# A transformer block with a Fourier mixer: the second norm of half the rows beside the feed-forward, the first norm's scale in the weights, another order of steps

## The chip, the cores and the metric

The kernel runs on one core of a Trainium2 chip. It is one launch; its time is the device time of that core in microseconds. The core's engines are TensorE (PE: matmuls, and loads of the stationary operand, PEld), VectorE (DVE), ScalarE (ACT), GpSimd (POOL) and SyncE (SP), which here only issues DMAs. Each works through its own list of instructions in order and waits on semaphores for the others. The compared number is the median of several runs; beside it there is one profiled execution, from which all durations below come.

## The reference

The block has 2048 rows (sequence) of 512 columns (hidden), and a feed-forward of 1792:

```python
mod = (silu(c) @ w_mod).reshape(1, 6, 1, -1)
sa, ca, ga, sb, cb, gb = (mod[:, i] for i in range(6))
h = layernorm(x) * (1 + ca) + sa
a = einsum("bsd,ed->bse", h, dft_hid_re); b = einsum("bsd,ed->bse", h, dft_hid_im)
y = einsum("ts,bse->bte", dft_seq_re, a) - einsum("ts,bse->bte", dft_seq_im, b)
x = x + ga * y
h = layernorm(x) * (1 + cb) + sb
out = (silu(h @ w1) * (h @ w3)) @ w2          # 512 -> 1792 -> 512
x = x + gb * out
```

All is fp32. The DFT matrices are inputs like the others.

## The kernel before

**Arithmetic.** Every matmul operand is split into a high part, rounded for TensorE's fast fp32 form, and a low rest (names ending in h and l), and a product is made of three passes: high by high, low by high, high by low. `product` (line 99) issues them. The DFTs use the matrices' mirror symmetry: sums and differences of mirrored rows and columns halve them. The matrices are inputs, so the kernel also compares the given matrices with the entries that it relies on; these are the "checks", whose loads are named cx, cy, cz, cv, and whose steps run beside other work; a general path behind a branch is there for other matrices and is not taken. The feed-forward's products are made with seven block products in place of eight: "units" a1 to a7 (w1) and b1 to b7 (w3) on the operands h2h, h2l and the block sums th, tl, and on block sums of the weights (w1s, w3s), each split again.

**Stages.** (1) The first layernorm of eight groups of row pairs k: statistics, scale, transposes by TensorE (`turn_rows`, line 712), then the modulation with 1 + ca and sa (`modulate_rows`, lines 725 and 727, on ACT or DVE: hm), mirror sums and differences (`mirror_sums`: hs, on DVE or POOL), their split (hh, hl), and the hidden DFT (`hid_product` line 805, `hid_difference` line 821), whose results are split into us and ul. (2) The sequence DFT (`seq_piece` line 1169, `seq_lines` line 1199) over four blocks of rows, with m, the matrix's pieces, split into mh and ml. The results of the odd and the even halves are read into od and ev; uv are the odd halves' sums. (3) For each of the four blocks: the gate ga, the additions to x (`odd_add`, `add_rows`: xa, xb), the statistics (`ln2_stats`), the root and scale (xn), transposes of x and of xn by TensorE into PSUM banks (`turn_block`, line 1346), a copy of the transposed x to DRAM (`keep_sums`: xm), and the modulation of the transposed xn (`modulate_block`: xc), from which h2h, h2l, th and tl are made. (4) The feed-forward: 14 items (g, pair), g a seventh of the 1792 columns, pair 0 the blocks 0 and 1, pair 1 the blocks 2 and 3; each item has 14 factor units and 8 down units of six matmuls of 512 columns, so 132 matmuls, 1848 in all. Beside each item ACT and DVE make silu and product (v, hf), read the down products (y), and split the next weights (w, w1s, w1l, w3s, w3sl and so on).

**What sets the order.** Stages 1 to 3 and the first units of 4 are `task`s: a name, a rank, needs, slots, and the engines that could do it, with a cost each. `arrange` is a list scheduler that runs when the program is built: again and again it takes, among the steps that could begin soonest by its own costs, the one of lowest rank. The tables `KIND_BY` and `STEP_BY` shift ranks by kind and by step. Large tiles lie in a pool of 50 slots; `take` gets the slot that was given back first, `give` returns one. From there on the loop over the items writes the order: units in a fixed pattern (a6, a5, y, y, ...), and behind each unit `beside` spends credits of DVE and ACT time on three queues, `jobs`, `background` and `checks`, in this order; `drain` works a queue off until something that is needed is there. The down products and other short uses of PSUM alternate between two banks. `look` starts the check loads (not with fewer than SPARE slots free, nor in paused items) and takes their steps LAG calls later.

## Time and profile before

| | us |
|---|---|
| median of 3 runs | 667.55 (666.27 to 671.1) |
| profiled execution | 672.04 |
| its span (first to last instruction) | 670.2 |
| mean granted TensorE clock in it | 0.958 |
| busy PE / DVE / ACT / POOL | 612.2 / 524.2 / 374.5 / 233.7 |

How to read the rows: a group's row names the line, the engine, the operation, output <- inputs, shapes and count, then busy time and mean duration in ns, then the engine's idle time ahead of the group and what ended it. A row of the chain of waits is start, duration, engine, output and line. A row of windows is the stretch, its length, then busy time and count of PE, PEld, DVE, ACT and POOL, the granted clock as a fraction, the DMA engines' busy share, and GB/s; where it is asked for one line of the program, only the engines that this line uses are there. "L99" is line 99 of the kernel.

### The profile page before, as it was taken

The page shows a single profiled execution, that of the slowest core. Times are in us where ns is not written, and L with a number is a line of the kernel's source. Part 1 is how long each engine was busy: PE and PEld are TensorE (multiplying, and loading weights), DVE is VectorE, ACT ScalarE, POOL GpSimd, SP SyncE. Part 2 cuts the span into 40 slices and gives each one's busy share as a digit, 9 for nine tenths or more (in the row PEclk, how much of TensorE's full clock was granted, in tenths as well). Part 3 has the DMA queues.
Part 4 walks back from the last instruction along what each step waited for, and adds up shares of the span by engine and source line. Part 5 has one row for each costly group of instructions (what it writes and reads, how often), then busy time and mean ns, then how long its engine had stood idle before and what let it go on. Part 6 is the DMA issues. An engine that isn't in the chain of part 4 may idle for free.

```text
span 670.2 us, 8742 instructions
## 1 busy us (share of the span) xinstructions
PE 612.2 (91%) x2893; PEld 500.4 (75%) x2893; DVE 524.2 (78%) x1014; ACT 374.5 (56%) x591; POOL 233.7 (35%) x252
## 2 busy tenths in 40 slices
PE   6989789999766989999999999997999999999975
PEld 3889778767544778778888888786878788887854
DVE  5898764999997655869787767797888899889462
ACT  5577564632558666465564757574656466565310
POOL 7875108248534014241522101321443335431000
PEclk7999998999769999999999999998999999999988
DMA  7662037943033529997999566898999999997004
GB/s 254 196 195 80 1 94 191 276 130 126 0 125 127 189 45 262 241 269 204 231 248 254 100 125 125 214 196 190 246 250 270 267 245 269 242 277 200 25 16 114
DMA packets 61872, 119.15 MB, mean 178 GB/s; under 512 B 10681, under 2 KB 29113, under 8 KB 61820
## 3 DMA queue, kind: packets, MB, share of 16 engines
q1 hardware_dynamic: 45228, 67.92, 35.5%
q0 software_dynamic: 13824, 47.98, 32.0%
q10 hardware_dynamic: 2768, 2.62, 1.3%
q8 instruction: 24, 0.39, 0.2%
q14 instruction: 28, 0.23, 0.1%
HBM read 85.99 MB, written 35.65 MB: 182 GB/s over the span
## 4 chain that ended last, share of the span: by engine, by line
PE 57%; DVE 16%; issue 8%; DMA 7%; ACT 6%; POOL 5%; SPq 0%; POOLq 0%; DVEq 0%; ACTq 0%
PE banks L99 40%; PE banks L1169 6%; DMA sum<-y 3%; PE banks L1199 2%; DMA cz<-in_ctr 2%; PE banks L821 2%; PE banks L805 1%; DMA w<-in_w 1%; DVE cj L1534 1%; DVE x L87 1%; POOL cy L273 1%; DMA lt<-dt 1%; PE banks L1346 1%; ACT th L81 1%; PE banks L1061 1%
## 5 line engine op out<-in xcount | busy, mean ns | idle before, releaser
L99 PE MATMUL banks<-hf,w2h 128*128 128x512 f32 (+1 forms) x452 | 142.5, 395 | 7.0 <-ACT hf L81 3.4
L1714 POOL DMA_DIRECT2D sum<-y x48 | 45.3, 953 | 216.9 <-ACT y L598 197.6
L99 PEld LDWEIGHTS banks<-hf,w2h 128*128 128x128 f32 x452 | 85.6, 191 | 28.5 <-DVE hf L84 4.3
L99 PE MATMUL banks<-hf,w2l 128*128 128x512 f32 (+1 forms) x226 | 88.6, 392 | 0.0
L598 ACT ACTIVATE y<-banks,gb 128x512 f32<-128x512 f32 x96 | 65.1, 682 | 20.8 <-PE banks L99 16.9
L81 ACT ACTIVATE hf<-v 128x512 fp32r<-128x512 f32 x56 | 35.4, 632 | 73.5 <-DVE v L90 67.8
L81 ACT ACTIVATE x<-banks 128x512 f32<-128x512 f32 x84 | 48.5, 590 | 21.8 <-PE banks L99 21.2
L87 DVE TENSOR_TENSOR x<-banks,x 128x512 f32<-128x512 f32 x42 | 28.9, 688 | 34.9 <-PE banks L99 28.2
L1798 ACT ACTIVATE v<-v 128x512 f32<-128x512 f32 x42 | 26.4, 629 | 49.8 <-DVE v L87 49.6
L99 PEld LDWEIGHTS banks<-hf,w2l 128*128 128x128 f32 x226 | 43.1, 191 | 8.7
L87 DVE TENSOR_TENSOR v<-banks,x 128x512 f32<-128x512 f32 x42 | 28.8, 687 | 17.7 <-PE banks L99 17.7
L84 DVE TENSOR_TENSOR hf<-v,hf 128x512 fp32r<-128x512 f32 x56 | 38.4, 685 | 2.5 <-ACT hf L81 2.3
L99 PE MATMUL banks<-tl,w1sh 128*128 128x512 f32 x84 | 33.3, 396 | 0.2 <-DVE tl L93 0.2
L99 PE MATMUL banks<-th,w1sh 128*128 128x512 f32 x84 | 33.2, 396 | 0.0
L99 PE MATMUL banks<-th,w1sl 128*128 128x512 f32 x84 | 33.2, 395 | 0.0
L99 PE MATMUL banks<-th,w3sh 128*128 128x512 f32 x84 | 32.9, 392 | 0.2 <-ACT x L81 0.2
L99 PE MATMUL banks<-th,w3sl 128*128 128x512 f32 x84 | 32.7, 389 | 0.0
L99 PE MATMUL banks<-tl,w3sh 128*128 128x512 f32 x84 | 32.7, 389 | 0.0
L90 DVE TENSOR_TENSOR v<-v,x 128x512 f32<-128x512 f32 x42 | 29.2, 695 | 1.4
L538 PE MATMUL banks<-tmp 128*128 128x128 f32 (+1 forms) x182 | 26.9, 300 | 3.1 <-DVE tmp L428 3.1
L805 PE MATMUL banks<-wu,hh 128*128 128x256 f32 x128 | 25.3, 296 | 3.7 <-ACT ho L81 2.4
L273 POOL DMA_INDIRECT cv<-in_cti,mirror x16 | 18.0, 1126 | 28.6 <-PE banks L99 23.9
(349 smaller groups left out, 1704.8 us busy)
## 6 DMA issues: line engine op xcount, KB each, us to landing
sum<-y POOLq DMA_DIRECT2D x48, 512.0 KB, 7.7
w<-in_w SPq DMA_DIRECT2D x42, 512.0 KB, 5.9
wmc<-in_wmc SPq DMA_DIRECT2D x8, 512.0 KB, 7.3
sum<-xm SPq DMA_DIRECT2D x8, 512.0 KB, 3.3
cx<-in_ctr SPq DMA_DIRECT2D x16, 256.0 KB, 10.1
cz<-in_ctr SPq DMA_DIRECT2D x16, 256.0 KB, 10.2
cx<-in_cti SPq DMA_DIRECT2D x16, 256.0 KB, 14.2
cz<-in_cti SPq DMA_DIRECT2D x16, 256.0 KB, 8.2
```

Of the source, the lines that this page charges most:

```text
L81: nc.scalar.activation(dst, src, AF.Copy, scale=scale)
L84: nc.vector.tensor_tensor(out=dst, in0=a, in1=b, op=OP.subtract)
L87: nc.vector.tensor_tensor(out=dst, in0=a, in1=b, op=OP.add)
L90: nc.vector.tensor_tensor(out=dst, in0=a, in1=b, op=OP.mult)
L99: nc.tensor.matmul(acc, lhs[a], rhs[b], start=first and n == 0, stop=last and n == len(PASSES) - 1, skip_group_check=more,)
L273: nc.gpsimd.indirect_dma_start(dst, None, src, bass.IndirectOffsetOnAxis(ap=at, axis=0))
L538: nc.tensor.matmul(warm[:, :width], onesf[:, :P], onesf[:, :width], start=True, stop=True)
L598: nc.scalar.activation(dst, src, AF.Identity, scale=by)
L805: nc.tensor.matmul(halves(hb[k])[:, m, :], sides((hh, hl)[a][k])[:, dt, m, :], wu[dt][:, b, m, :], start=False, stop=dt % 2 == 1 and n == ...
L1169: nc.tensor.matmul(acc(b, m), (mh, ml)[p][b, o][:, m, cols(a)], (us, ul)[q][k][:, m, :], start=(o, a, n) == (0, 0, 0), stop=False, skip_gr ...
L1714: nc.gpsimd.dma_start(sums[t, d // 2], y, accum_op=OP.add)
L1798: behind(k != 0 or q == 0, lambda: nc.scalar.activation(v, src, AF.Silu))
```

## The change

Five things are changed together.

*Order.* `take` gets the slot that comes free earliest by the planner's time, and `arrange` reckons with it: a step that needs a slot is not planned before the soonest slot is left. `drain` charges costs. Both tables of ranks are new (23 kinds in place of 45, 18 steps in place of some 60).

*First norm.* The scale 1 + ca goes into the hidden DFT's weights: `w_highs`, `w_lows` and the new `round_differ` multiply by a column of mod1. The shift sa becomes a row: `shift_product`, eight matmuls of 97 x 512, a few small splits (qs, qt), and `hid_shift` and `hid_share` add it into the hidden DFT's banks; the side products of lines and rows get a term each. `modulate_rows` is gone; `own_rows` copies one half of the transposed rows from PSUM, and `mirror_sums` takes the other from PSUM, on DVE alone.

*Second norm's sums.* `add_rows` runs as scalar_tensor_tensor on 512 columns with an accumulated sum; the mean is taken from it, ACT squares the centred row with a second sum, and the root divides by D. `ln2_stats` is gone.

*Blocks 2 and 3.* Their norm, from the loads of the rows to the modulated transposes, is a list of steps in `background`, beside the first items. Transposes go in groups of four, each into the next of the two down banks, and ACT reads them.

*Checks.* LAG is 7 instead of 9, SPARE 7 instead of 6 and two more until block 3 is done; loads pause in item 6 alone, not in 5 and 6.

The first place is TensorE at the end of the sequence DFT. Before, the last of L1199 is followed by transposes and a few units (L99):

```order
L1199 MATMUL banks<-ya_243,er_1283 128x512
L1199 MATMUL banks<-ya_243,sel_329 128x512
...
L1346 MATMUL banks<-ident,xn_1819 128x128 x2
L1346 MATMUL banks<-anti,xn_1821 128x128 x2
L99 MATMUL banks<-h2h_1854,w1h_1564 128x512
...
L1346 MATMUL banks<-ident,xa_1649 128x128 x2
L1346 MATMUL banks<-anti,xb_1650 128x128 x2
L99 MATMUL banks<-th_2060,w1sh_1598 128x512
```

After, the normalized rows of block 1 (xn) are turned ahead of the last piece (L1256, L1286), and only transposes of x (xa, xb) and the first units (L106) follow:

```order
L1435 MATMUL banks<-ident,xn_1691 128x128 x2
L1435 MATMUL banks<-anti,xn_1708 128x128 x2
L1256 MATMUL banks<-us_921,mh_1640 128x512
...
L1286 MATMUL banks<-ya_244,er_1226 128x512
L1286 MATMUL banks<-ya_244,sel_323 128x512
...
L1435 MATMUL banks<-anti,xb_1181 128x128 x2
L106 MATMUL banks<-h2h_1749,w1h_1570 128x512
...
L106 MATMUL banks<-h2h_1763,w1l_1597 128x512
L1435 MATMUL banks<-ident,xa_1384 128x128 x2
```

The transposes of xn of blocks 0 and 1 have moved ahead of the end; of blocks 2 and 3 none is left here.

The second place is the third item of the feed-forward, on TensorE and ScalarE (th, tl, h2h, h2l are operands of factor units, hf of down units). On TensorE block 2's transposes now stand between the units:

```order
L106 MATMUL banks<-tl_1892,w3sh_2371 128x512
L106 MATMUL banks<-th_1888,w3sl_2373 128x512
L1435 MATMUL banks<-ident,xn_2451 128x128 x2
L1435 MATMUL banks<-anti,xn_2462 128x128 x2
L106 MATMUL banks<-hf_2336,w2h_2238 128x512 x2
...
L106 MATMUL banks<-hf_2290,w2l_2240 128x512
L1435 MATMUL banks<-ident,xn_2451 128x128 x2
L1435 MATMUL banks<-anti,xn_2462 128x128 x2
L106 MATMUL banks<-th_1896,w3sh_2371 128x512
...
L106 MATMUL banks<-th_1896,w3sl_2373 128x512
L1435 MATMUL banks<-ident,xn_2451 128x128 x2
L1435 MATMUL banks<-anti,xn_2462 128x128 x2
L106 MATMUL banks<-h2h_1749,w1h_2412 128x512
```

On ScalarE the root of block 2, with a load of its table ahead and another behind the modulations, now stands among x, y, hf and v of the feed-forward:

```order
L88 ACTIVATE hf_2487<-v_2299 128x512
L621 ACTIVATE y_2489<-banks,gb 128x512
L1414 ACT_TABLE_LOAD
L1414 ACTIVATE ln_2383<-ln_2383,eps 128x4
L88 ACTIVATE x_2460<-banks 128x512
L88 ACTIVATE x_2516<-banks 128x512
...
L1467 ACTIVATE xc_2568<-banks,sb,cb_234 128x512 x2
L1929 ACT_TABLE_LOAD
L1929 ACTIVATE v_2563<-v_2563 128x512
```

Before, no transpose of a second norm and no table load stands in this item; the one load stood ahead of the first v. The third place is ScalarE at the end of the hidden DFT. Before, the copy ho of the last pair stands behind two pieces mh and their squares (junk):

```order
L81 ACTIVATE mh_1112<-m_922 128x1024
L81 ACTIVATE mh_1123<-m_1107 128x1024
L294 ACTIVATE junk_1136,chk<-mh_1123 128x512 x2
L294 ACTIVATE junk_1147,chk<-ec_934 128x1024
L81 ACTIVATE ho_1159<-banks 128x512
```

After, the second of these mh stands behind it:

```order
L88 ACTIVATE ho_1069<-banks 128x512
L88 ACTIVATE mh_1074<-m_859 128x1024
...
L88 ACTIVATE ho_1134<-banks 128x512
L88 ACTIVATE gr_1139<-banks 64x64 x2
L88 ACTIVATE us_1144<-banks 128x2x256
L88 ACTIVATE us_1168<-banks 128x2x256
L88 ACTIVATE mh_1187<-m_1085 128x1024
```

The diff, cut to its core; the two tables stand as one line of the new one, since their numbers say nothing to a reader:

```diff
     def take(dt=F32, what="s"):
-        slot = free.popleft()
+        slot = min(free, key=lambda n: left_at[n])
+        free.remove(slot)
+        taken.append(left_at[slot])
         count[0] += 1
         t = big.tile([P, 2, N], dt, name=f"{what}_{count[0]}", tag=f"slot{slot}")
         slot_of[id(t)] = (slot, t)
         return t
 
-    def give(t):
+    def give(t, after=0.0):
         slot, _ = slot_of.pop(id(t))
         free.append(slot)
+        left_at[slot] = now[0] + after
+        given.append((slot, after))
...
+            soonest = sorted(left_at[n] for n in free)
...
+                        if slots and us:
+                            begin = max(begin, soonest[0])
...
+            fn(engine) if len(ways) > 1 else fn()
+            if taken and us and max(taken) > begin:
+                begin = max(taken)
+                put(begin)
+                for slot, more in given:
+                    left_at[slot] = now[0] + more
...
-        for m, sign in enumerate((1.0, -1.0)):
-            copy(u[:, 0, m, :], r[:, m, 0, :], sign)
+        for m in range(2):
+            copy_by(u[:, 0, m, :], r[:, m, 0, :], mod1[:, 1 + m, dt : dt + 1])
...
+    def round_differ(dt):
         r = quarters(raw_w[dt])
         if dt % 2 == 0:
             wd[dt // 2] = take(F32R, "wd")
...
+        for m in range(2):
+            copy_by(
+                wd[dt // 2][:, dt % 2, m * HALF : (m + 1) * HALF], r[:, m, 1, :],
+                mod1[:, 1 + m, dt : dt + 1],
+            )
...
+    def shift_product(m, dt):
+        nc.tensor.matmul(
+            bank(6)[:97],
+            mod1[:, 0, dt : dt + 1].to_broadcast([P, 97]),
+            raw_w[dt][:, m, :],
+            start=dt == 0,
+            stop=dt == ND - 1,
+        )
...
-    def modulate_rows(k, dt, engine):
-        if k not in hm:
-            hm[k] = take(F32, "hm")
-        src = turned[k][dt // 2][:, (dt % 2) * HALF : (dt % 2 + 1) * HALF]
-        dst = four(hm[k])[:, dt, :]
-        sa, ca1 = mod1[:, 0, dt : dt + 1], mod1[:, 1, dt : dt + 1]
-        if engine == "ACT":
-            nc.scalar.activation(dst, src, AF.Identity, bias=sa, scale=ca1)
-        else:
-            nc.vector.tensor_scalar(dst, src, ca1, sa, op0=OP.mult, op1=OP.add)
-
-    def mirror_sums(k, m, engine):
-        if k not in hs:
-            hs[k] = take(F32, "hs")
-        own = sides(hm[k])[:, :, 0, :]
-        dst = sides(hs[k])[:, :, m, :]
-        tensors(engine, dst, own, sides(hm[k])[:, :, 1, :], OP.subtract if m else OP.add)
-        if k == NK // 2:
-
-            (nc.gpsimd if engine == "POOL" else nc.vector).tensor_copy(sides(hs[k])[:, :, m, 0:1], own[:, :, 0:1])
+    def turned_rows(k):
+        return banks[:, 2 * (k % 2) : 2 * (k % 2) + 2, :].rearrange(
+            "p h (t s n) -> p (h t) s n", t=2, s=2
+        )
+
+    def own_rows(k):
+        hs[k] = take(F32, "hs")
+        copy(sides(hs[k])[:, :, 0, :], turned_rows(k)[:, :, 0, :])
+
+    def mirror_sums(k, m):
+
+        first = int(k == NK // 2)
+        own = sides(hs[k])[:, :, 0, :]
+        mirrored = turned_rows(k)[:, :, 1, first:]
+        (minus if m else plus)(sides(hs[k])[:, :, m, first:], own[:, :, first:], mirrored)
+        if m and first:
+            nc.vector.tensor_copy(sides(hs[k])[:, :, 1, 0:1], own[:, :, 0:1])
...
+    def hid_shift(k, first):
+
+        nc.tensor.matmul(
+            hb[k], shift_twos(k), shift_row[:, 0, :], start=first, stop=False, skip_group_check=True
+        )
...
+    def hid_share(k, m, n):
+        nc.tensor.matmul(
+            halves(hb[k])[:, m, :], shift_ones(1) if m else shift_twos(k), shift(n),
+            start=False, stop=False, skip_group_check=True,
+        )
...
-    def add_rows(b, n, engine):
-        t = ev[b][:, n : n + 1, :].to_broadcast([P, 2, N])
-        tensors(engine, xrow[b][n], xrow[b][n], t, OP.add)
-        if n:
+    def add_rows(b, n, q):
+
+        if (n, q) == (0, 0):
+            ln[b] = small.tile([P, 4, 4], F32, name=f"ln_{b}", tag="ln")
+        row = xrow[b][n][:, q, :]
+        nc.vector.scalar_tensor_tensor(
+            row, ev[b][:, n, :], 1.0, row, op0=OP.mult, op1=OP.add,
+            accum_out=ln[b][:, 0, 2 * n + q : 2 * n + q + 1],
+        )
+        if (n, q) == (1, 1):
...
-    def ln2_stats(b, n):
-        if n == 0:
-            ln[b] = (
-                small.tile([P, 4, 2], F32, name=f"lmv_{b}", tag="lmv"),
-                small.tile([P, 2, 4], F32, name=f"lrs_{b}", tag="lrs"),
-            )
-        st = small.tile([P, 6], F32, name=f"lst_{b}_{n}", tag="st")
-        nc.vector.bn_stats(st, xrow[b][n // 2][:, n % 2, :])
-        nc.vector.bn_aggr(ln[b][0][:, n, :], st)
+    def ln2_mean(b):
+        nc.vector.tensor_scalar(ln[b][:, 1, :], ln[b][:, 0, :], -1.0 / D, None, op0=OP.mult)
+
+    def ln2_square(b, n):
+        if n % 2 == 0:
+            xn[b, n // 2] = take(F32, "xn")
+        nc.scalar.activation(
+            xn[b, n // 2][:, n % 2, :], xrow[b][n // 2][:, n % 2, :], AF.Square,
+            bias=ln[b][:, 1, n : n + 1], scale=1.0, accum_out=ln[b][:, 2, n : n + 1],
+        )
 
     def ln2_root(b):
-        mv, r = ln[b]
-        nc.scalar.activation(r[:, 0, :], mv[:, :, 1], AF.Sqrt, bias=eps, scale=1.0)
+        r = ln[b]
+        nc.scalar.activation(r[:, 2, :], r[:, 2, :], AF.Sqrt, bias=eps, scale=1.0 / D)
...
+    def block_steps(b, next_bank):
+
+        def run(slots, dve, act, fn, *args):
+            step(background, slots, lambda: fn(*args), dve, act)
+
+        run(6, 0.0, 0.0, load_rows, b)
+        background.extend([PAUSE] * 4)
+        for n in range(2):
+            run(1 - n, 0.7, 0.0, odd_pair, b, n, "DVE")
+        run(0, 1.2, 0.0, odd_gates, b, "DVE")
+        for n in range(2):
+            run(0, 0.7, 0.0, odd_add, b, n, "DVE")
+        run(0, 1.2, 0.0, all_gates, b, "DVE")
+        if b == NT - 1:
+            run(0, 0.0, 0.0, lambda: give(gar.pop(0)))
+        for n in range(4):
+            run(0, 0.8, 0.0, add_rows, b, *divmod(n, 2))
+        run(0, 0.2, 0.0, ln2_mean, b)
+        for n in range(4):
+            run(3 - n, 0.0, 0.7, ln2_square, b, n)
+        run(0, 0.0, 0.3, ln2_root, b)
+        run(0, 0.3, 0.0, ln2_inverse, b)
+        for n in range(4):
+            run(0, 0.0 if n % 2 else 0.6, 0.8 if n % 2 else 0.0, ln2_scale, b, n, ("DVE", "ACT")[n % 2])
+        for what in "nx":
+            for i in range(2):
+                for q in range(2):
+                    to = []
+
+                    def turn_one(what=what, i=i, q=q, to=to):
+                        to.append(next_bank())
+                        turn_block(b, what, i, q, to[0])
+
+                    def read_one(what=what, i=i, q=q, to=to):
+                        (keep_sums if what == "x" else modulate_block)(b, i, q, to[0])
+
+                    run(1 - q, 0.0, 0.0, turn_one)
...
+                    run(1 - q, 0.0, 0.8 if what == "n" else 0.6, read_one)
...
+        "add": 3, "check": -16, "eq": 51, "ex": -13, "gr": 6, "gtt": 56, "hl": 9, "jw": -7,
...
+            task(f"qm{m}.{dt}", r + dt, ["modr", f"w{dt}", *before], lambda m=m, dt=dt: shift_product(m, dt), PE=0.93)
...
-        task(f"wh{dt}", -8 + 2 * dt - 26.6, [f"w{dt}"], lambda dt=dt: w_highs(dt), 1, ACT=0.73)
+        task(f"wh{dt}", -8 + 2 * dt - 26.6, [f"w{dt}", "modr"], lambda dt=dt: w_highs(dt), 1, ACT=0.83)
...
-    for b in range(NT):
-        r = begun + (24 if b < 2 else 48) + 3 * (b % 2)
+    for b in range(2):
+        r = begun + 24 + 3 * b
...
+    for b, what in ((0, "n"), (1, "n"), (0, "x"), (1, "x")):
+        r = begun + 24 + 3 * b + (30 if what == "x" else 0)
+        for i in range(2):
+            pair = 4 if (what, i) == ("n", 0) else 6
+            needs = [f"add{b}.{n}" for n in range(4)] if what == "x" and not i else [f"sc{b}.{n}" for n in range(4)]
+            needs += pair_of.get(pair, ["rowr1"] if pair == 4 else ["yc", "rowr5"])
...
-    LAG, AHEAD, SPARE = 9, 6, 6
+    LAG, AHEAD, SPARE = 7, 6, 7
     clock, begun_at, paused = [0], {}, []
+
+    def spare():
+        return SPARE if ("xc", NT - 1) in done else SPARE + 2
 
     def look(force=False):
         clock[0] += 1
-        while to_load and "lt" in done and not paused and (len(free) > SPARE or force) and len(begun_at) < AHEAD:
+        while to_load and "lt" in done and not paused and (len(free) > spare() or force) and len(begun_at) < AHEAD:
...
+    def next_bank():
+        turn[1] += 1
+        return bank(down_banks[(turn[1] - 1) % len(down_banks)])
+
+    for b in range(2, NT):
+        block_steps(b, next_bank)
...
-        paused[:] = [i] if turning - 2 <= i < turning else []
+        paused[:] = [i] if turning - 1 <= i < turning else []
```

349 lines of the change are left out of this document (193 added, 156 removed), and 17 rows, old and new, of the table STEP_BY.

## The prediction

> **What bounds the kernel now.** I read the page's head first, then the busy time of each engine in four stretches cut where the work changes, then the chain of waits around the cuts.
>
> ```profile
> span 670.2 us, 8742 instructions
> ...
> PE 612.2 (91%) x2893; PEld 500.4 (75%) x2893; DVE 524.2 (78%) x1014; ACT 374.5 (56%) x591; POOL 233.7 (35%) x252
> ```
>
> ```profile
> core 0: us, PE busy (x) PEld busy (x) DVE busy (x) ACT busy (x) POOL busy (x), PEclk, DMA share, GB/s
> 0.00:175.20 175.20, 157.93 (x903) 131.43 (x903) 142.03 (x292) 97.32 (x179) 95.70 (x131) 0.94 0.52 148
> 175.20:220.07 44.87, 28.19 (x137) 22.03 (x137) 36.81 (x51) 31.41 (x40) 17.02 (x8) 0.77 0.30 108
> 220.07:662.50 442.43, 426.09 (x1853) 346.94 (x1853) 345.23 (x672) 245.80 (x373) 121.02 (x113) 0.99 0.81 198
> ```
>
> PE (TensorE) is busy 91% of the span. Up to 175.20 us stand the first norm, the hidden DFT and the sequence DFT; from 220.07 us to 662.50 us stands the feed-forward, where PE hardly rests. Between them lie 44.87 us in which PE is busy for 28.19 us, and at a granted clock of 0.77. The same stretches for the feed-forward's matmuls alone (line 99), then for the transposes of the second norm alone (line 1346), say what PE did there:
>
> ```profile
> 175.20:220.07 44.87, 9.15 (x25) 5.52 (x25) 0.77 0.30 108
> 220.07:662.50 442.43, 423.54 (x1829) 343.96 (x1829) 0.99 0.81 198
> ```
>
> ```profile
> 0.00:175.20 175.20, 1.09 (x8) 0.86 (x8) 0.94 0.52 148
> 175.20:220.07 44.87, 20.56 (x112) 16.63 (x112) 0.77 0.30 108
> 220.07:662.50 442.43, 1.25 (x8) 0.92 (x8) 0.99 0.81 198
> ```
>
> Only 25 feed-forward matmuls are done in the gap; 112 of the 128 transposes are. The chain of waits has the price of both at full clock, and what opens the feed-forward:
>
> ```profile
> 155.08 1.02 PE banks L1346 x8
> ...
> 218.80 1.24 DVE tl L93
> ...
> 299.84 125.68 PE banks L99 x552
> ```
>
> A transpose is 1.02/8 = 0.128 us, a feed-forward matmul 125.68/552 = 0.2277 us. So the gap holds 25 x 0.2277 + 112 x 0.128 = 20 us of PE work in 44.87 us. The rest are waits for the DVE (VectorE) and ACT (ScalarE), as the PE's timeline shows (idle time ahead in brackets), and the clock that goes down with them:
>
> ```profile
> 178.29 0.47 PE L1346 MATMUL banks<-ident,xn 128*128 128x128 f32 x1 [3.12 <-DVE xn L1340]
> ...
> 191.44 0.79 PE L99 MATMUL banks<-h2l,w1h 128*128 128x512 f32 x1 [3.48 <-DVE h2l L93]
> ```
>
> **The gap.** After the change blocks 2 and 3 have no second norm here, and on PE the 32 normalized transposes of blocks 0 and 1 stand before the end of the sequence DFT (rows of the PE order above). What is left for PE between that end and the steady feed-forward is 32 transposes of x, 32 x 0.128 = 4.1 us, and the 25 matmuls, 5.7 us. I add 3 us for waits: two of the x groups reuse a bank pair that ACT must copy first, a copy of about 1 us as the ACT row at 214.36 us below shows, and the first operand once more. That makes 12.8 us where 44.87 us stood: **-32.1**. The 24 transposes (32, where 8 stand now) that go into the sequence DFT lengthen it by 24 x 0.128: **+3.1**.
>
> This needs the DVE to be ready. These groups stand on it between the hidden DFT and the feed-forward:
>
> ```profile
> L1315 DVE BATCH_NORM_STATS2 lst<-xa 128x6 f32<-128x512 f32 x8 | 5.4, 672 | 0.0
> L1315 DVE BATCH_NORM_STATS2 lst<-xb 128x6 f32<-128x512 f32 x8 | 5.3, 663 | 0.0
> L1316 DVE BATCH_NORM_AGGREGATE lmv<-lst 128x2 f32<-128x6 f32 x16 | 2.9, 182 | 0.6
> L93 DVE TENSOR_TENSOR xb<-xb,ev 128x1024 f32<-128x1024 f32 x4 | 7.0, 1762 | 0.1
> L93 DVE TENSOR_TENSOR xa<-xa,ev 128x1024 f32<-128x1024 f32 x2 | 4.6, 2298 | 0.7 <-POOL ev L93 0.6
> L1340 DVE TENSOR_SCALAR xn<-xb,lrs 128x512 f32<-128x512 f32 x4 | 2.1, 542 | 0.1
> L607 DVE SCALAR_TENSOR_TENSOR wmc<-wmc,scr 128x512 f32<-128x512 f32 x16 | 12.6, 824 | 5.5 <-PE banks L1061 5.2 <-DMA wmc<-in_wmc 0.3
> ```
>
> All of the first five go, 25.2 us. Instead come 8 additions with a sum as by-product for blocks 0 and 1. The trace has no such form with an accumulator; the nearest is line 607's at 0.824 us, so 6.6 us. That is 18.6 us less. Of nine scalings like line 1340's six stay, 1.6 us less: about 20 us. If the DVE alone set the pace, the feed-forward would open near 200 us. But it was idle for 44.87 - 36.81 = 8.1 us in the gap itself, waiting for others, and the xa and xb additions took 1.8 to 2.3 us while POOL (GpSimd) worked beside them, which the new form, on DVE alone, shortens. So I take PE's sum and keep 20 us as the other end.
>
> **Beside the feed-forward.** 64 transposes go in and 8 come out: 56 x 0.128 = **+7.2**, since PE is full there. They come in 16 groups of four; each takes a bank of the down products and must be read by ACT before the bank is free. The nearest groups of four now are line 1484's, four of them; the dearest are line 1346's, eight groups for xn:
>
> ```profile
> L1484 PE MATMUL banks<-ident,dl 128*128 128x128 f32 x16 | 2.8, 294 | 1.8 <-ACT y L598 1.2 <-ACT dt L81 0.7
> L1346 PE MATMUL banks<-ident,xn 128*128 128x128 f32 x32 | 8.3, 343 | 10.0 <-ACT xm L81 3.4 <-DVE xn L1340 3.1 <-ACT xc L1375 2.2
> ```
>
> That is 1.8/4 = 0.45 us or 10.0/8 = 1.25 us a group, or nothing where the bank has long been read: 0 to 20 us. The groups are placed between units, with 6 to 12 matmuls (1.4 to 2.7 us) to the next use, so I take half of the nearest row: **+3.6**.
>
> The root now splits the feed-forward's activations, with two table loads for each of blocks 2 and 3. The one load at the start of the feed-forward reads:
>
> ```profile
> 214.36 1.02 ACT L81 ACTIVATE xm<-banks 128x1024 f32<-128x1024 f32 x1 [0.24 <-PE banks L1346]
> 215.41 1.28 ACT L1798 ACT_TABLE_LOAD   x1
> 216.70 0.63 ACT L1798 ACTIVATE v<-v 128x512 f32<-128x512 f32 x1
> ```
>
> Four loads are 5.1 us of ACT, of which it has 442.43 - 245.80 = 197 us free; but an x, a y or a silu queued behind a load is late by 1.28 us, and PE waits for those. I take 0.5 us each: **+2**, ends 0 and 5.1. [...]
>
> The rest of the two blocks' norm lies over the first five items (5 x 132 x 0.2277 = 150 us). By the forms above it is about a dozen DVE instructions of 0.55 to 1.2 us a block, some 9 us, and as many on ACT, some 10 us. The DVE's 97 us of idle time between 220 and 662 us and ACT's 197 us are the cover. If it is gone, the DVE's 18 us show. The changed lag, spare slots and pause of the loads I cost at nothing: they act on idle times of the kind below.
>
> **The start.** The first norm's modulation goes:
>
> ```profile
> L725 ACT ACTIVATE hm<-banks,mod 128x256 f32<-128x256 f32 x18 | 9.1, 556 | 3.1 <-DVE hm L727 2.9 <-PE banks L712 0.2
> L727 DVE TENSOR_SCALAR hm<-banks,mod 128x256 f32<-128x256 f32 x14 | 7.2, 537 | 0.9 <-issue 0.5 <-ACT hm L725 0.3
> L81 ACT ACTIVATE ho<-banks 128x512 f32<-128x512 f32 x8 | 4.8, 596 | 3.0 <-PE banks L805 2.7
> L93 DVE TENSOR_TENSOR hs<-hm 128x512 f32<-128x512 f32 x11 | 7.8, 718 | 0.2
> L538 PE MATMUL banks<-tmp 128*128 128x512 f32 x6 | 4.5, 902 | 3.1 <-DVE tmp L428 3.1
> ```
>
> ACT loses 9.1 us and gains 8 copies like the third row's, 4.8 us, and 8 roundings of weight differences, by the first row's 0.556 us at most 4.4 us; the DVE loses 7.2 us and gains five mirror sums that POOL did, 5 x 0.718 = 3.6 us. The eight shift products are fp32 with 512 columns, as the last row's, and so at most 8 x 0.9 = 7.2 us of PE, but they stand where the same line 538 now fills PE's waits. The weights' high parts have to wait for the modulation vector now. And one knot is undone. Here ACT waits for a DMA with the odd DFT piece's mh and holds back the hidden product's copy ho; PE then stands:
>
> ```profile
> 93.81 1.06 ACT L81 ACTIVATE mh<-m 128x1024 fp32r<-128x1024 f32 x1 [3.87 <-DMA m<-in_cti]
> ...
> 97.95 0.50 PE L805 MATMUL banks<-wu,hh 128*128 128x256 f32 x2 [2.19 <-ACT ho L81]
> ```
>
> In the new ACT order that copy comes ahead of that mh. Between +7 us (the shift products' 7.2 us all on the path) and -11 us (the DVE's 7.2 us of modulation and the 3.87 us of the wait, both whole) I take **-4**, nearest to the knot.
>
> **Sum.** The profiled execution took 672.04 us, 0.67% over the 667.55 us median. 672.0 - 4 - 32.1 + 3.1 + 7.2 + 3.6 + 2 = 651.8 us; times 667.55/672.04, **647 us** as a median.
>
> **The rivals.** *The feed-forward pays it back.* Each group waits 1.25 us and each load is bare: 672.0 - 4 - 32.1 + 3.1 + 7.2 + 20 + 5.1 = 671.3, as median 667 us. For it: ACT is in order, and one row of it holds root, scales, modulation and reads behind each other. Against it: line 1484's groups. Chance 0.15.
>
> *The DVE sets the start.* The gap shrinks by 20 us only: 672.0 - 4 - 20 + 3.1 + 7.2 + 3.6 + 2 = 663.9, as median 659 us. For it: the DVE has 36.81 us of the gap's 44.87. Chance 0.13.
>
> *The start gives 11 us, and the late weight load shown below goes too*, 3.7 us, since loads pause in one item instead of two: 672.0 - 11 - 32.1 + 3.1 + 7.2 + 3.6 + 2 - 3.7 = 641.1, as median 637 us. For it: the first stage hangs on chains through ACT and DVE, and both get shorter. Against it: neither is busy all of the time there, so a saving need not show. Chance 0.13.
>
> *Late weights: slower.* What PE waits for in the middle of the feed-forward, and the DVE's wait behind it:
>
> ```profile
> PE banks L99 <- DVE x L87: 3.7, 1, 3.7
> ```
>
> ```profile
> 456.34 0.42 DVE L93 TENSOR_TENSOR w3s<-w 128x256 f32<-128x256 f32 x1 [3.17 <-DMA w<-in_w]
> ```
>
> ```profile
> 460.00:480.00 20.00, 20.00 (x83) 16.34 (x82) 17.75 (x40) 11.53 (x18) 6.63 (x6) 0.91 1.00 224
> ```
>
> The new code keeps two more slots back from the check loads until block 3 is done and puts two blocks' rows, six slots each, beside the weights; the DMA is at 0.81 of its time there. If a weight comes late in each of the first seven items, PE loses 3.7 us and, at clock 0.91 over 20 us, 1.8 us more: 5.5 x 7 = 38 us, giving 690 us, as median 685 us. It decides from (672.0 - 651.8)/7 = 2.9 us an item. Against it: one such wait is all the present trace has, and it lies where the loads were paused for two items. Chance 0.06.
>
> *It does not do what it says*, the blocks' norm being drained in one piece: the order has its transposes one group at a time between units. Chance 0.01, at the first rival's time.
>
> **Numbers.** The likeliest case has 0.52. The range runs from 632 us (the third rival without its 3.6 us of bank waits and 2 us of loads) to 664 us (the first rival but for its last 3 us). About 1%, some 6.7 us, is what a measurement here can tell from no change: faster is below 660.9 us, slower above 674.2 us. Faster: 0.52 + 0.13 of the third rival + 0.09 of the second, which lies close to the bound, + 0.06 of the first = 0.80; same: the rest, 0.14; slower: 0.06.
>
> **What would show it.** The steady feed-forward should begin some 9 to 13 us after the last sequence line product, near 180 us, with the granted clock at 1.0 between them; 16 groups of transposes should stand in the feed-forward with less than 0.5 us of PE idle time each; four more table loads of 1.28 us; no batch-norm statistics after the first norm's; the copy ho of the last pair without the DMA wait ahead of it. [...] I would be wrong if PE waits for the DVE's tl as at 218.80 us, or if the wait for y and x beside the new groups adds up to more than 20 us.

## The result, and the profile after

| | before | after |
|---|---|---|
| median | 668.66 us (666.27 to 671.1, 4 runs) | 710.09 us (709.3 to 714.24, 4 runs) |
| ratio, 95% interval | | 1.0632 (1.0572 to 1.0691) |
| profiled execution | 672.04 us | 710.69 us |
| its span, granted clock | 670.2 us, 0.958 | 708.9 us, 0.948 |

The change makes the kernel 6.3% slower; 647 us was forecast. Below, "before" without more is the kernel before, measured on the same chip as the run beside it. Two lines of the profile's page of after come first, and then its windows, cut at the last sequence line product and at the steady feed-forward:

```profile
span 708.9 us, 8674 instructions
...
PE 626.9 (88%) x2865; PEld 502.9 (71%) x2865; DVE 522.4 (74%) x1003; ACT 390.9 (55%) x631; POOL 221.9 (31%) x244
```

```profile
0.00:182.26 182.26, 162.23 (x900) 131.05 (x901) 147.59 (x284) 111.17 (x208) 86.49 (x123) 0.94 0.45 128
182.26:193.79 11.53, 7.37 (x47) 5.78 (x46) 8.21 (x9) 7.26 (x8) 6.19 (x3) 1.00 0.63 210
193.79:702.40 508.61, 457.31 (x1921) 366.10 (x1921) 366.57 (x712) 272.51 (x416) 129.22 (x119) 0.95 0.73 183
```

The gap did what the forecast said: 11.53 us at clock 1.00 where 44.87 us stood. The stage ahead of it ends 7.06 us later (182.26 for 175.20). The loss is in the feed-forward: 508.6 us for 442.4. PE's idle time in it is 508.61 - 457.31 = 51.3 us, for 442.43 - 426.09 = 16.3 us before, and the clock is 0.95 where it was 0.99. The rows below say what PE waits for there: the engine and line waited for, then the total, the number of waits and the longest in us:

```profile
PE banks L106 <- ACT hf L88: 11.6, 3, 5.6
PE banks L106 <- ACT x L88: 10.4, 7, 3.2
PE banks L1435 <- DVE xn L1430: 7.6, 2, 4.0
PE banks L1435 <- ACT xc L1467: 5.9, 4, 1.5
PE banks L1435 <- ACT xm L88: 4.5, 3, 1.9
```

The three rows of line 1435 are the transposes of blocks 2 and 3: 18.0 us. The other two, hf and x, are the feed-forward's own. The waits of DVE and ACT in the feed-forward say what stands behind these; neither row is in the same list of before:

```profile
DVE cj L1665 <- DMA cy<-in_ctr,mirror: 20.9, 5, 5.3
ACT hf L88 <- DMA sum<-y: 12.0, 2, 6.3
```

The first row holds checks whose indirect load has not landed. They stand on DVE ahead of the sums and products x and v, from which ACT makes hf; and in ACT's list y and x come behind that hf. So a check, which nobody is in a hurry for, stops PE. One of the five is shown here on DVE, ACT and PE in turn:

```profile
502.10 1.19 DVE L1665 SCALAR_TENSOR_TENSOR cj<-cx,cy 128x992 f32<-128x992 f32 x1 [5.35 <-DMA cy<-in_ctr,mirror]
```

```profile
506.47 0.63 ACT L88 ACTIVATE hf<-v 128x512 fp32r<-128x512 f32 x1 [5.30 <-DVE v L97]
507.00 0.67 ACT L621 ACTIVATE y<-banks,gb 128x512 f32<-128x512 f32 x1
507.57 0.59 ACT L88 ACTIVATE x<-banks 128x512 f32<-128x512 f32 x1
```

```profile
508.21 0.79 PE L106 MATMUL banks<-th,w3sh 128*128 128x512 f32 x1 [3.18 <-ACT x L88]
```

The second row is hf's slot: `take` gave one whose last tile, a y, the DMA had not yet added to its sum in DRAM. Its longest wait, 6.3 us, ends at 654.90 us, and PE's longest for hf, 5.6 us, ends behind it at 655.59 us.

**A group's wait, step by step.** ScalarE of after, at the root of block 3:

```profile
341.43 0.71 ACT L1407 ACTIVATE xn<-xb,ln 128x512 f32<-128x512 f32 x1
342.04 0.19 ACT L1407 ACTIVATION_READ_ACCUMULATOR xn<-xb,ln 128x1 f32 x1
342.25 1.28 ACT L1414 ACT_TABLE_LOAD   x1
343.55 0.30 ACT L1414 ACTIVATE ln<-ln,eps 128x4 f32<-128x4 f32 x1
...
348.95 0.69 ACT L621 ACTIVATE y<-banks,gb 128x512 f32<-128x512 f32 x1 [1.18 <-PE banks L106]
349.54 0.77 ACT L1467 ACTIVATE xc<-banks,sb,cb 128x512 f32<-128x512 f32 x1
```

DVE behind it, and PE, which stood at the transposes from 340.94 us:

```profile
343.87 0.18 DVE L1418 RECIPROCAL ln<-ln 128x4 f32<-128x4 f32 x1 [1.66 <-ACT ln L1414]
...
344.29 0.55 DVE L1430 TENSOR_SCALAR xn<-xa,ln 128x512 f32<-128x512 f32 x1
```

```profile
344.98 0.67 PE L1435 MATMUL banks<-ident,xn 128*128 128x128 f32 x2 [4.04 <-DVE xn L1430]
350.36 0.69 PE L1435 MATMUL banks<-ident,xn 128*128 128x128 f32 x2 [1.45 <-ACT xc L1467]
358.63 0.44 PE L1435 MATMUL banks<-ident,xn 128*128 128x128 f32 x2 [1.51 <-ACT xc L1467]
```

The sum, the table load, the root, the reciprocal and the scaling are issued back to back, and PE's list has the transposes right behind: 4.04 us. The later groups wait for their bank. The two banks of the down products are used in turn by units (read as y) and groups (read as xc), and the xc of one group is issued behind the next y: 0.69 + 0.77 = 1.46 us, about what PE waits in the last two rows.

### The profile page after: what moved, and what is told of

Its sections match the earlier page's. It is cut to its first block, busy times and chain, and to the rows that moved or that the text cites. A ratio compares the mean times of both kernels' runs of the same rounds, so it can differ in the third digit from the quotient of the medians.

```text
span 708.9 us, 8674 instructions
## 1 busy us (share of the span) xinstructions
PE 626.9 (88%) x2865; PEld 502.9 (71%) x2865; DVE 522.4 (74%) x1003; ACT 390.9 (55%) x631; POOL 221.9 (31%) x244
## 5 line engine op out<-in xcount | busy, mean ns | idle before, releaser
L106 PE MATMUL banks<-hf,w2h 128*128 128x512 f32 (+1 forms) x452 | 147.2, 407 | 18.7 <-ACT hf L88 11.6
L106 PEld LDWEIGHTS banks<-hf,w2h 128*128 128x128 f32 x452 | 87.7, 197 | 40.9 <-ACT hf L88 12.8
L106 PE MATMUL banks<-hf,w2l 128*128 128x512 f32 (+1 forms) x226 | 90.8, 402 | 0.0
L106 PEld LDWEIGHTS banks<-hf,w2l 128*128 128x128 f32 x226 | 44.6, 197 | 9.3
L106 PE MATMUL banks<-th,w3sh 128*128 128x512 f32 x84 | 35.4, 422 | 9.7 <-ACT x L88 9.7
L106 PE MATMUL banks<-th,w1sh 128*128 128x512 f32 x84 | 34.9, 416 | 1.5 <-ACT th L88 0.8
L106 PE MATMUL banks<-tl,w1sh 128*128 128x512 f32 x84 | 34.4, 409 | 1.1 <-DVE tl L100 1.1
L106 PE MATMUL banks<-th,w3sl 128*128 128x512 f32 x84 | 34.7, 413 | 0.0
L1665 DVE SCALAR_TENSOR_TENSOR cj<-cx,cy 128x992 f32<-128x992 f32 x16 | 19.1, 1191 | 21.1 <-DMA cy<-in_ctr,mirror 20.9
L106 PE MATMUL banks<-tl,w3sh 128*128 128x512 f32 x84 | 34.5, 411 | 0.0
L106 PE MATMUL banks<-th,w1sl 128*128 128x512 f32 x84 | 34.3, 408 | 0.0
L106 PEld LDWEIGHTS banks<-th,w3sh 128*128 128x128 f32 x84 | 16.6, 198 | 15.7 <-ACT x L88 12.4
```

What stands on the lines that cost most here:

```text
L106: nc.tensor.matmul(acc, lhs[a], rhs[b], start=first and n == 0, stop=last and n == len(PASSES) - 1, skip_group_check=more,)
L1665: nc.vector.scalar_tensor_tensor(out, a, by, b, op0=OP.mult, op1=OP.not_equal, accum_out=at)
```

## The experiments

Two theories of the 63 us between forecast and result. **A, the checks:** the lag of 7 calls, with the other spare slots and the shorter pause, lets DVE wait for loads. **B, the distance:** blocks 2 and 3's steps stand too close to each other for engines that work in order. A rival to both: the move itself, or its table loads, is what costs.

**1. The old rules of the checks.**

```diff
-    LAG, AHEAD, SPARE = 7, 6, 7
+    LAG, AHEAD, SPARE = 9, 6, 6
...
-        return SPARE if ("xc", NT - 1) in done else SPARE + 2
+        return SPARE
...
-        paused[:] = [i] if turning - 1 <= i < turning else []
+        paused[:] = [i] if turning - 2 <= i < turning else []
```

> The changed kernel with the three old rules for the checks: a check's steps 9 calls behind its load instead of 7, 6 spare slots instead of 7 and 9, loads paused in two items instead of one. Theory A (the shorter lag puts the check steps ahead of their data, and VectorE, in order, stands before them: 20.9 us of waits for cy, and behind them TensorE): the five waits for cy go, TensorE's waits at the turn of the items (3.18, 2.24, 1.94, 0.83, 1.20 and 5.55 us, 15 us) mostly go with them and with their lost clock, and the time falls by 15 to 25 us, to 685 to 695 us. Theory B (the norm of blocks 2 and 3 beside the feed-forward costs it all): no more than 5 us.

Measured: 694.45 us, 1.0392 (1.0325 to 1.0459) of before. About 16 us of the loss go, and with them the checks' wait for cy. PE's own waits change more than they shrink: in the profiled execution, the slowest of the four, PE waits 1.4 us for ACT's x where it waited 10.4, but 11.8 us for DVE's x where it waited 0.4; and ACT stands 10.3 us at one x whose slot a y's DMA still reads. Which of the three rules gives the 16 us, this run does not say.

**2. The kernel before with the new lag alone.**

```diff
-    LAG, AHEAD, SPARE = 9, 6, 6
+    LAG, AHEAD, SPARE = 7, 6, 6
```

> The kernel before, with the lag of the check steps set to 7 instead of 9 and nothing else. Theory A: VectorE waits for the checks' data here too, by 10 to 20 us, and the time rises by 8 to 20 us, to 676 to 688 us. The rival (the loads come late only because of what else the changed kernel puts on the queues): the wait stays near the 1 to 3 us of now and the time within 3 us.

Measured: 684.14 us, 1.0262 (1.0189 to 1.0334). Both waits appear in a kernel that has nothing else of the change:

```profile
DVE cj L1534 <- DMA cy<-in_ctr,mirror: 18.8, 7, 4.0
ACT hf L81 <- DMA sum<-y: 13.3, 3, 7.0
```

So the lag alone, a single number, costs 2.6%, some 17 us by the ratio and 14 us by the medians (684.14 for 670.09), where nothing else is changed. The interval lies clear of no change: A holds for its part.

**3. No table loads.** The square root of blocks 2 and 3 is left out: the identity, which needs no load, stands in its place.

```diff
-            nc.scalar.activation(r[:, 2, :], r[:, 2, :], AF.Sqrt, bias=eps, scale=1.0 / D)
+            nc.scalar.activation(r[:, 2, :], r[:, 2, :], AF.Sqrt if b < 2 else AF.Identity, bias=eps, scale=1.0 / D)
```

> The changed kernel with the root of blocks 2 and 3 left out (the same instruction with the identity instead of the square root), so that ScalarE loads no table for it: four loads of 1.28 us fewer, all else in place. If the loads hold up the chain root, scale, transposes: TensorE's waits for xn (3.58 and 4.04 us) shrink by about 1.3 us each, and with what is queued behind the loads the time falls by 4 to 10 us. If they only fill idle time of ScalarE: less than 2 us.

Measured: 705.1 us, 1.0553 (1.0484 to 1.0621), some 5 us less than after. The two intervals overlap; the runs' own times do not (702.45 to 705.66 us, and 709.3 to 714.24 us). Four loads of 1.28 us are 5.1 us, so each may be paid whole, as the forecast's upper end had it; but they are not what costs the 63 us.

**4. Distance.** A pause is an empty step: one unit of PE's work goes by. Two go ahead of the root, one between root and scaling, two ahead of the first transposes, one behind each group; and each group's read is issued right behind its transposes, ahead of the next y.

```diff
+        background.extend([PAUSE] * 2)
         run(0, 0.0, 0.3, ln2_root, b)
+        background.extend([PAUSE])
         run(0, 0.3, 0.0, ln2_inverse, b)
...
+        background.extend([PAUSE] * 2)
         for what in "nx":
...
-                    run(1 - q, 0.0, 0.0, turn_one)
-                    run(1 - q, 0.0, 0.8 if what == "n" else 0.6, read_one)
+                    run(1 - q, 0.0, 0.8 if what == "n" else 0.6, both_one)
+                    background.extend([PAUSE])
```

> The changed kernel with the steps of blocks 2 and 3 further apart: two units between the squares and the root, one behind the root, two between the scales and the first transposes, one behind each group of transposes, and ScalarE's read of a group issued right behind the group instead of behind the next down product. Theory B (TensorE reaches the transposes before their operands, and finds the down bank still unread behind a y): the waits of 22.8 us between 281 and 396 us and the lost clock go, and the time falls by 20 to 35 us, to 675 to 690 us. Theory A alone: no more than 5 us.

Measured: 673.09 us, 1.0074 (1.0034 to 1.0115), 37 us less than after, with no matmul, no transpose and no table load taken away. PE's waits of line 1435 shrink from 18.6 us (its rows above and 0.6 us) to 2.3 us:

```profile
PE banks L1435 <- ACT xn L1428: 0.9, 3, 0.3
PE banks L1435 <- ACT xm L88: 0.7, 1, 0.7
PE banks L1435 <- ACT xc L1467: 0.7, 1, 0.7
```

and the checks' wait for cy is nearly gone too, though the lag is still 7:

```profile
DVE cj L1672 <- DMA cy<-in_cti,mirror: 0.5, 1, 0.5
```

**5. Both.** The spaced steps with LAG 9.

> The changed kernel with the steps of blocks 2 and 3 spaced as in the run before and the lag of the check steps back at 9; spare slots and pause as changed. If the two costs are separate, the 37 us of the spacing and most of the 16 us of the old rules for the checks add up: 655 to 662 us, faster than the kernel before by 1% to 2%. If they are one cost seen twice (late data either way): within 5 us of the spacing alone, 668 to 673 us.

Measured: 670.92 us, 1.0006 (0.9968 to 1.0045). The some 657 us that runs 1 and 4 would give together (710 - 37 - 16) do not come; against run 4 the lag is worth 0.7%, the difference of the ratios, and their intervals overlap. The last row of run 4 says why: with the steps spaced the checks no longer waited. So run 4's 37 us hold most of A's 16 us, and, reckoned so, some 21 us are B's own. How the spacing takes it wasn't tried; the steps of the checks come last of the three queues, so a longer list ahead of them moves them. The slot's wait is not gone with the lag: ACT's hf stands 13.5 us for a y's DMA in run 5 (19.9 us in run 4), and PE still waits 11.1 us for hf. So the lag is not that wait's only cause.

**6. The rows earlier.** In run 5 the addition of block 2 still waits on DVE for the rows' load, as in after (6.2 us there):

```profile
DVE xa L100 <- DMA xa<-in_x: 8.2, 1, 8.2
```

```diff
         run(6, 0.0, 0.0, load_rows, b)
-        background.extend([PAUSE] * 4)
+        background.extend([PAUSE] * 12)
```

> The same with the rows of each block loaded twelve units ahead of their first use instead of four. In the spaced run VectorE waited 8.7 us for the rows xa of block 2, with TensorE waits of 2.04 and 2.39 us behind it. If those come from the late load: 3 to 6 us faster than without this. If the slots that the rows then hold longer delay the weights: 0 to 5 us slower.

Measured: 661.34 us, 0.9876 (0.9822 to 0.993). The wait is gone and 1.3 points of ratio with it, more than expected, and the kernel is 1.2% faster than before, with an interval clear of no change. Most of the gain is clock: of the 12.0 us between the two profiled spans, 9.4 us are PE's busy time, which falls from 613.0 to 603.6 us for the same 2865 matmuls, at a clock of 0.975 where run 5 had 0.960. One wait stands out now, in the last item:

```profile
638.16 0.80 PE L106 MATMUL banks<-hf,w2h 128*128 128x512 f32 x1 [13.11 <-ACT hf L88]
```

There the loop forces all checks that are left, and then the verdict on them, onto DVE ahead of hf: 10 us of check steps from 621.73 us, and 4 us of the verdict's.

**7 and 8. Two parts of the start,** each on run 5: the six fills of the shift row as a later step of ACT; and hl wholly on DVE instead of partly on POOL.

```diff
-    shift_begin()
...
+    task("qz", 15, [], shift_begin, ACT=2.2)
...
```

> Spacing and lag 9, and the six copies on ScalarE that prepare the shift row are issued behind the first group's work instead of ahead of the first root. In the trace of the changed kernel they stand for 2.2 us there, and the first root begins 2.2 us later than before. If the start of the first stage is a chain through ScalarE: 1.5 to 2.5 us faster than the run with spacing and lag 9. If another wait takes over: within 1 us.

```diff
-            task(f"hl{k}", r + RANK["hl"], [f"hh{k}"], lambda e, k=k: sum_lows(k, None, e), 1, DVE=1.22, POOL=2.4)
+            task(f"hl{k}", r + RANK["hl"], [f"hh{k}"], lambda k=k: sum_lows(k, None, "DVE"), 1, DVE=1.22)
```

> Spacing and lag 9, and the low parts of the first norm's mirror sums (hl, 1024 columns) all on VectorE instead of six on GpSimd. In the changed kernel VectorE's instructions beside GpSimd's are stretched (a weight rest of 0.48 us took 5.05 us while GpSimd ran two long ones). If that stretching costs the first stage more than the 1.2 us of VectorE that each hl takes: the sequence DFT ends 2 to 5 us earlier and the time falls by as much. If VectorE's own time is what is short: 2 to 6 us slower.

Measured: 670.64 us, 1.0028 (0.9992 to 1.0064), and 672.36 us, 1.0032 (0.9995 to 1.0069), for run 5's 1.0006. Neither shows a gain. In both the last sequence product begins earlier than in run 5's profiled execution (180.08 and 179.52 us for 182.31), but that says little: in the other executions with run 5's first stage (after and runs 1, 3, 4, 6, 9, 10 and 11) it begins anywhere from 179.11 to 181.77 us. In run 7 PE's wait ahead of the first transposes is 3.56 us, where after, with run 5's first stage, has 5.01 us, and the next one, for DVE's x, 4.44 us, where it has 4.07 us. In run 8 that second wait is gone, but the planner, given another way for hl, wrote another order, and PE waits behind the sequence DFT instead; the feed-forward's matmuls behind this wait last 0.63 us each in their rows from 192.44 to 194.57 us, and 0.39 us from 195.91 us on:

```profile
190.25 0.69 PE L1435 MATMUL banks<-ident,xa 128*128 128x128 f32 x2 [3.70 <-ACT xm L88]
```

**9. The move undone.** LAG 9, and the steps of blocks 2 and 3 worked off in one piece ahead of the second item.

```diff
+    held_back = list(background)
+    background.clear()
     for b in range(2, NT):
         block_steps(b, next_bank)
+    while background:
+        _, *cost, fn = background.popleft()
+        if fn is not None:
+            fn()
+    background.extend(held_back)
```

> The changed kernel with the lag back at 9, and with the second norm of blocks 2 and 3 done in one piece ahead of the second item instead of step by step between units: the move beside the feed-forward is undone, everything else of the change stays. Against the run with the lag alone at its old value there is none, so the bounds are the 694 us of the old check rules and the 671 us of the spaced steps with lag 9. If steps without distance between units are what costs the time, a piece of its own costs about half of the old gap's waits (25 us for four blocks, so 12 us for two) and some 4 us for the rows' load, where the steps beside the feed-forward lost some 33 us with the clock: 675 to 685 us. If the move pays and only the checks' lag did harm, undoing it gives back the 32 us of the gap's term in part, and the time is above 694 us.

Measured: 703.09 us, 1.0518 (1.0483 to 1.0553). Two waits of PE hold 36.4 us, where the steps beside the feed-forward waited 18.6 us:

```profile
223.93 0.66 PE L1435 MATMUL banks<-ident,xn 128*128 128x128 f32 x2 [17.62 <-DVE xn L1430]
249.56 0.66 PE L1435 MATMUL banks<-ident,xn 128*128 128x128 f32 x2 [18.74 <-DVE xn L1430]
```

The expectation put half of the old gap's waits there and missed: the old order overlapped four blocks, one piece here waits through each of its chains. And the edit takes the pauses behind the rows' loads out with the other empty steps, so DVE stands 3.41 and 13.22 us for them:

```profile
239.93 0.69 DVE L100 TENSOR_TENSOR xa<-xa,uv 128x512 f32<-128x512 f32 x1 [13.22 <-DMA xa<-in_x]
```

With the same lag, this piece is 5 points of ratio above run 5, where the steps stand spaced beside the feed-forward; but DVE's waits for the loads are 16.6 us of these some 34, so it speaks against the rival in part only. What speaks against it most are runs 4 to 6: the move stays in them, and their times lie 0.7% above that of before, level with it and 1.2% under it.

**10 and 11. The last item's wait,** both on run 6: spare slots 7 throughout; and spare slots 6 (8 until block 3 is done) with no pause of the check loads.

```diff
-        return SPARE if ("xc", NT - 1) in done else SPARE + 2
+        return SPARE
```

> Steps spaced, lag 9, rows asked for early (661 us), and the spare slots 7 throughout instead of 9 until block 3 is done. The loads for the checks then start earlier: 4 groups of checks are left in front of the verdict in the last item, where 11 were. If the 13.11 us for which TensorE waits there for hf are these checks on VectorE, about 7 x 1 us of them go and the time is near 654 us. If they are only where another wait shows (the last weights or sums), the time stays at 661 us; if the spare slots were needed for the weights, waits for x in the middle appear and the time is 665 us or more.

```diff
-    LAG, AHEAD, SPARE = 9, 6, 7
+    LAG, AHEAD, SPARE = 9, 6, 6
...
-        paused[:] = [i] if turning - 1 <= i < turning else []
+        paused[:] = []
```

> Steps spaced, lag 9, rows early (661 us), spare slots 6 after block 3 and 8 before, and no pause of the check loads in any item. 2 groups of checks are left in front of the verdict. If checks spilled into the last item are its wait, the time is near 652 us; if the pause protected the weights of the item where the pairs change, a wait of 3 to 6 us for x moves there and the time is 656 to 661 us.

Measured: 672.65 us, 1.0092 (1.0065 to 1.012), and 660.95 us, 0.9894 (0.9877 to 0.991). In both the last wait shrinks as fewer checks are left there, from 13.11 us to

```profile
648.91 0.80 PE L106 MATMUL banks<-hf,w2h 128*128 128x512 f32 x1 [6.75 <-ACT hf L88]
```

in run 10, and to

```profile
637.04 0.79 PE L106 MATMUL banks<-hf,w2h 128*128 128x512 f32 x1 [5.01 <-ACT hf L88]
```

in run 11, so the checks were most of that wait; the verdict's 4 us stay in both. But the gain is spent elsewhere. In run 10 PE waits 12.7 us for DVE's x in six places, where run 6 has one such wait of 3.2 us. The longest, and its cause on ACT:

```profile
248.41 0.80 PE L106 MATMUL banks<-th,w3h 128*128 128x512 f32 x1 [4.61 <-DVE x L94]
```

```profile
247.04 0.60 ACT L88 ACTIVATE x<-banks 128x512 f32<-128x512 f32 x1 [9.40 <-DMA sum<-y]
```

It is the slot again: with fewer slots kept back from the check loads before block 3 is done, the next one in turn is still being read by a y's DMA. Run 11 holds 8 back there and keeps run 6's time.

**12. Runs 7 and 8 together on run 11.**

> The run without any pause of the check loads (660.95 us: spaced steps, lag 9, rows early, spare slots 6 and 8), with two things of the start besides, each of which alone changed nothing that can be told from none: the six fills of the row of shifts as a later step of ScalarE's, and hl wholly on VectorE. If each of them was covered by the wait that the other leaves (the fills by VectorE's stretched x, hl by the first norm's root), the two together shorten the start by the 2 to 5 us that the profiles of the single runs show at the end of the sequence DFT, and the time is 656 to 659 us. If the start is held by something third, the time stays within 1.5 us of 661 us.

Measured: 662.67 us, 0.9924 (0.9898 to 0.9949): no gain, nearest to "something third". PE's idle time up to 105 us falls from 17.7 to 12.4 us against run 11 (3.8 us of this is only fill: 38 more of line 564's matmuls, whose results nobody reads), and between 105 and 200 us it rises from 5.6 to 9.1 us. One wait of 3.75 us, that of run 8 again, stands where run 11 has 1.11 us, and ACT's rows say why: the copy that frees the bank now stands behind three copies of another operand.

```profile
189.65 0.69 PE L1435 MATMUL banks<-ident,xa 128*128 128x128 f32 x2 [3.75 <-ACT xm L88]
```

```profile
185.74 2.95 ACT L88 ACTIVATE th<-xc 128x1024 fp32r<-128x1024 f32 x3 [0.58 <-DVE xc L100]
188.60 1.00 ACT L88 ACTIVATE xm<-banks 128x1024 f32<-128x1024 f32 x1
```

An order found for one set of times does not keep its other end when a part is made shorter.

## Why the prediction was wrong, point by point

The sum of the forecast with what was measured, on the profiled executions:

| term | forecast | measured | from |
|---|---|---|---|
| start | -4 | +4.0 | 182.26 - 175.20 - 3.1 |
| 24 transposes in the sequence DFT | +3.1 | +3.1 | kept |
| gap | -32.1 | -33.3 | 11.53 for 44.87 |
| 11 more matmuls behind it | 0 | +2.5 | 14 stand in the gap, not 25; 0.2277 each |
| 56 transposes | +7.2 | +7.2 | kept |
| waits at line 1435 in the feed-forward | +3.6 | +17.6 | 18.6, less 1.0 before |
| PE's other waits there | +2 | +17.4 | 32.7 for 15.3 |
| clock there | 0 | +21 | 508.61 x 0.05 - 442.43 x 0.01 |
| sum | 651.8 | 711.5 | profiled 710.69 |

**The gap** was right, in size and in its reason: PE's own sum set it (7.4 us of work, and 4.2 us of waits where 3 were taken), and the clock stayed at 1.00 in it. The rival in which DVE sets the start did not come. The new additions cost DVE about what was taken for them, 0.824 us: one is 0.68 us, and 0.08 us more for its sum.

```profile
330.37 0.68 DVE L1392 SCALAR_TENSOR_TENSOR xb<-ev,xb 128x512 f32<-128x512 f32 x1
330.98 0.08 DVE L1392 DVE_READ_ACCUMULATOR xb<-ev,xb 128x1 f32 x1
```

**"So I take half of the nearest row: +3.6"** is the first step that failed. The 16 groups waited 18.6 us, 1.16 us each, close to the dearest row that the forecast had quoted (1.25 us), and over the 0.5 us that it named as its sign. The forecast took "6 to 12 matmuls to the next use" for distance. On PE it is; but the read of a group stood on ACT behind the y of the next unit, and the root's chain had no distance at all. The order of ACT, which the forecast had in hand, shows both. Run 4 confirms it: the same instructions with distance wait 2.3 us there.

**"The changed lag, spare slots and pause of the loads I cost at nothing"** is the second. The lag is a promise that a load has landed when DVE, which is in order, comes to its check. In after the loads of cy take a median of 8.5 us (in_ctr) and 9.5 us (in_cti) from issue to landing; by an estimate from a matmul's 0.2277 us, seven units of six matmuls are 9.6 us and nine are 12.3 us, so the new lag lies close to these medians and the old one some 3 us above them. Run 2 prices the lag alone at 2.6%, run 1 the three numbers at about 16 us in the changed kernel; the checks' 20.9 us above are what PE's longest waits for x go back to. The slot's 12.0 us, which stand behind the longest wait for hf, come with the lag in run 2 (13.3 us) and stay without it in run 5 (13.5 us), so their cause is open in part. The fourth rival came near it (waits in the middle items, through DVE, on late loads), but it took the weights for late, where check loads and slots were, and had 0.06.

**Two table loads for each of two blocks, "+2"**: about 5 us by run 3, near the upper end. Each of the loads takes 1.28 us in the rows, and block 3's has no further time around it: the root starts at 343.55 us, 0.02 us behind its load, and the load 0.02 us behind the instruction ahead of it (342.04 + 0.19).

**The clock** had no term. The waits of 35 us beyond before's came with 21 us of lost clock, by the table's estimate from the lengths and clocks of the two windows. PE's busy time agrees: 457.31 - 426.09 = 31.2 us more, of which the added matmuls and transposes are 2.5 + 7.2. The forecast used that effect in one rival alone (3.7 us of wait, 1.8 us of clock), where the first rival's 25 us of waits, and the sum's own, needed it too.

**The start** was mis-sized by some 8 us. Two of its parts came as forecast: the knot is undone (PE waits 0.5 us for ho, where it waited 2.4), and the shift products (7.7 us of PE busy time in 16 instructions) stand where line 538 filled PE's waits, which has 106 matmuls of 15.1 us left (line 564 of after) where it had 176 of 22.4 us. But PE's idle time up to the cut rises by 2.8 us, with waits ahead of the first norm's transposes: 5.01 us for 3.31 at the first of them, and 4.07 us for an x that DVE scales behind its step of 5.05 us (last section). One and the same first stage ends up to 3 us apart from execution to execution, so the 8 us are known no better than to some 3. Runs 7, 8 and 12 took these waits up without a gain; which chain holds the start stays open.

**The rivals.** The first, "the feed-forward pays it back", had the right place and the right price for the groups and the loads; it stopped at 667 us since it knew neither the checks' part nor the clock, and kept the start's -4 us. The range's upper end of 664 us was this rival's, and so fell with it.

**What was worth having:** with the steps spaced, the old lag and the rows early, the changed kernel takes 661 us, 1.2% under before. The expected 647 us are not reached; the start's 8 us are one part of what lies between, and waits such as run 6's 13.11 us in the last item another.

## What to carry to other kernels

When work moves into a full stage, count not only its instructions but the distance between each step and the one that needs it, on every in-order engine that it passes: a chain of short steps issued back to back (sum, table load, root, reciprocal, scaling: 2.5 us by their rows) held TensorE for 4.04 us here. A constant that stands for "landed by then" is part of the path as soon as an in-order engine with urgent work consumes the load; a change to it must be priced like a wait (here two calls fewer cost 2.6% in run 2). And in this kernel waits of TensorE cost more than their length: 35 us more of them came with 21 us of clock, by the estimate above, so here a term for waits needed a term for the clock beside it.

## What the runs showed of the hardware that was not expected

The clock was near half behind a wait of 2.24 us, and at 1.00 behind one of 3.2 us. In after, TensorE waits 2.24 us until 542.29 us, and these windows (length, PE busy and count, clock, DMA share, GB/s) show 0.54 for the 3 us from 543 us:

```profile
542.29 0.74 PE L106 MATMUL banks<-th,w3sh 128*128 128x512 f32 x1 [2.24 <-ACT x L88]
```

```profile
540.00:543.00 3.00, 0.76 (x3) 0.90 1.08 310
543.00:546.00 3.00, 3.00 (x9) 0.54 1.01 315
546.00:549.00 3.00, 3.00 (x14) 1.00 0.90 208
```

In run 11 a wait of 3.44 us for an x of DVE is followed by a clock of 0.50, in run 6 one of 3.2 us at the same place by 1.00:

```profile
445.00:450.00 5.00, 4.46 (x11) 0.50 0.81 172
```

```profile
443.00:448.00 5.00, 4.20 (x18) 1.00 0.76 169
```

So the length of the wait alone does not decide it in these three; what does was not shown.

And one step of DVE took some ten times its median beside work of POOL: line 655's eight instructions of 256 columns take 0.45 to 5.05 us, with a median of 0.476. The long one is one of the two in the row below, while POOL makes sel and hl:

```profile
29.07 5.44 DVE L655 SCALAR_TENSOR_TENSOR wu<-w,mod,wu 128x256 fp32r<-128x256 f32 x2
```

```profile
29.43 2.08 POOL L1197 TENSOR_SCALAR sel<-st,signs 64x512 fp32r<-64x512 f32 x1
31.49 2.33 POOL L100 TENSOR_TENSOR hl<-hs,hh 128x1024 fp32r<-128x1024 f32 x1
```

It ends at 34.51 us, with POOL at work until 33.82 us. Beside sel's other instructions (20.23 to 26.70 us) six of the eight ran in about 0.5 us each. In run 8, with hl on DVE, PE no longer waits for the x behind that step (4.07 us in after), and the kernel gains nothing.
